# Two heads of a pair on row and column halves of the PE array, in place of a block-diagonal q and full-array numerators

## The chip, the cores and the metric

The kernel runs on one core of one Trainium2 chip. The metric is the time of one execution on the device in microseconds (us), lower is better. Engines are named as the profile names them: PE is TensorE (matmuls), PEld its weight loads, DVE is VectorE, ACT is ScalarE, POOL is GpSimd, SP is SyncE. All runs compared here are of the state that the measurement calls fast. Each kernel was run next to the kernel before on the same chip, and the comparison is by the ratio of the two.

## The reference, cut to what matters

Eight batches of eight heads, 576 tokens, head width 64. Attention is a band of 32 tokens to each side plus 8 global tokens; behind it comes an MLP with a snake activation.

```python
B, H, S, D = 8, 8, 576, 64                         # n_global = 8, window = 32
scores = q @ k^T / sqrt(D)                         # masked: |i-j| <= 32, or i or j global
attn   = softmax(scores)
x      = (attn @ v) as (B*S, 512)
h      = x @ w_in                                  # 512 -> 2048
g      = h + sin(alpha*h)**2 / alpha
out    = g @ w_out                                 # 2048 -> 512
```

## The kernel before

Work goes in chunks. For chunk `p` an *attention stretch* computes batch `p`, and carries the second-MLP matmuls (64 of 512 columns) of the chunk before as filling. Then a *first-MLP stretch* computes `w_in` and the activation for chunk `p`; it also holds the transposes of k and q for the first two head pairs of the next batch. An attention stretch has eight units: four head pairs `hp` times two halves `hf` of the sequence. A half has `NU` = 6 windows of `QC` = 56 query columns (48 own, 8 global) against 128 key rows.

Both heads of a pair (2 x 64 rows) share one matmul on the full 128 x 128 array. Scores need the heads apart, so q is stored block-diagonally (`qBD`: head 0 in rows 0 to 63, zeros below it, and so on), and ACT fills it with two 64-partition copies:

```python
for t in range(2):                                  # stage_T: q of one head pair
    pr = slice(64 * t, 64 * t + 64)
    nc.scalar.copy(out=qBD[hp][pr, :, t, 0:QB], in_=Qps[pr]...)

for u in range(NU):                                 # stage_Q: scores, 6 matmuls of 112 columns
    nc.tensor.matmul(out=Sp[:, u // HU, o : o + 2 * QC],
                     lhsT=kTw[hp][:, hf * NU + u, :], rhs=qBD[hp][:, hf * NU + u, :, :], ...)
E = exp(Sp) on ACT; E *= MASK on DVE

for t, on in enumerate((ones0, ones1)):             # stage_D: 2 accumulating matmuls of 336
    nc.tensor.matmul(out=den, lhsT=on[:], rhs=E[.., t, :], start=(t == 0), stop=(t == 1))
lnd = Ln(den); rec = Exp(-lnd) on ACT; gd = sum of den's global columns on DVE

num = psA.tile([P, 2, CH], F32, name="num")         # stage_V: two PSUM banks
for u in range(NU):                                 # 6 matmuls of 112 columns
    nc.tensor.matmul(out=num[:, u // HU, o : o + 2 * QC],
                     lhsT=W[:, .., hp * P : (hp + 1) * P], rhs=E[:, u // HU, o : o + 2 * QC], ...)
for t in range(2):                                  # the useful half of num, head by head
    nc.vector.tensor_tensor(out=xT[pr, hp, ...], in0=numv[pr, :, :, t, 0:QB], in1=rec[pr]..., op=mult)
nc.vector.tensor_reduce(out=gn, in_=numv[..., QB:QC], op=add)
```

The order of issue:

```python
# for each unit j: first(j) = scores(j+2), denominators(j+1); second(j) = numerators(j)
counts = [2, 0, 1, 0] + [1, 0] * NUN    # MLP slots (4 matmuls) behind each first/second
# next batch's transposes, as extras of the first-MLP slots 10 and 13:
i_ = (10, 13)
```

The matmuls write to eight banks of PSUM, the accumulator memory: two are held throughout (`Kps`, `ops`); the other six are shared in turn by the attention tiles and by the six `hb` tiles of the first MLP.

The softmax here doesn't subtract the row's maximum and nothing guards it: scores larger than these inputs give would overflow.

Of the kernel before, what the change touches and what calls it, by code (L numbers as in the profile page):

```python
# [12 lines left out]
ALU = mybir.AluOpType  # L13
# [5 lines left out]
def kernel(  # L19
# [11 lines left out]
    nc = tc.nc  # L31
    P = 128
    BF = DT.bfloat16
    F32 = DT.float32
# [32 lines left out]


    identb = const.tile([P, P], BF, name="identb")
    ones0 = const.tile([P, P], BF, name="ones0")  # L70
    ones1 = const.tile([P, P], BF, name="ones1")
    MASK = const.tile([P, NW, QC], BF, name="MASK")
    w_in = const.tile([P, CT, DFF], BF, name="w_in")
    w_out = const.tile([P, NT, DM], BF, name="w_out")
# [1 line left out]
    recipT = const.tile([P, NT], F32, name="recipT")  # L76
    xT = const.tile([P, CT, NTOK], BF, name="xT")
    kTw = [const.tile([P, NW, P], BF, name=f"kTw{i}") for i in range(NHP)]
    qBD = [const.tile([P, NW, 2, QC], BF, name=f"qBD{i}") for i in range(NHP)]
    VW = [const.tile([P, 2, NU, DM], BF, name=f"VW{i}") for i in range(2)]  # L80
    GT = const.tile([P, 2, NHP, B, NG], BF, name="GT")
    VgN = const.tile([NG * B, DM], BF, name="VgN")
# [63 lines left out]
    def zero(ap):  # L146
        nc.vector.memset(ap, 0.0)
# [52 lines left out]

    for hp in range(NHP):
        zero(kTw[hp][:, :, KB:P])
        zero(qBD[hp][:].rearrange("p i t c -> p (i t c)").bitcast(F32))
    zero_v(1)
    zero(ones0[:])
    zero(ones1[:])
    nc.vector.memset(ones0[:, 0:64], 1.0)
    nc.vector.memset(ones1[:, 64:128], 1.0)

    gN = [setup.tile([NG * B, DM], F32, name=f"gN{i}") for i in range(3)]  # L210
    halves = ((nc.sync, range(0, NG // 2)), (nc.scalar, range(NG // 2, NG)))
# [84 lines left out]
    def globals_in(b, hp, eng=nc.gpsimd):  # L296
        eng.tensor_copy(
            out=kTw[hp][:, :, KB : KB + NG],
            in_=GT[:, 0, hp, b, None, :].to_broadcast([P, NW, NG]),
        )  # L300
        for t in range(2):
            pr = slice(64 * t, 64 * t + 64)
            eng.tensor_copy(
                out=qBD[hp][pr, :, t, QB:QC],
                in_=GT[pr, 1, hp, b, None, :].to_broadcast([64, NW, NG]),
            )

    def stage_T(b, hp, qpool, qtag):
        QS, KS = qk[b]
        for jt in range(NTW):  # L310
            nc.tensor.transpose(
                out=Kps[:, WIN + jt * TW : WIN + (jt + 1) * TW],
                in_=KS[:, jt, 2 * hp : 2 * hp + 2, :],
                identity=identb[0:TW, 0:TW],
            )
        base = Kps[:, 0:1]
        nc.vector.tensor_copy(
            out=kTw[hp][:, :, 0:KB],
            in_=bass.AP(
                tensor=base.tensor, offset=base.offset,  # L320
                ap=[list(base.ap[0]), [QB, NW], [1, KB]],
            ),
        )
        Qps = qpool.tile([P, S], BF, name=qtag)
        for jt in range(NTW):
            nc.tensor.transpose(
                out=Qps[:, jt * TW : (jt + 1) * TW],
                in_=QS[:, jt, 2 * hp : 2 * hp + 2, :],
                identity=identb[0:TW, 0:TW],
            )  # L330
        for t in range(2):
            pr = slice(64 * t, 64 * t + 64)
            nc.scalar.copy(  # L333
                out=qBD[hp][pr, :, t, 0:QB],
                in_=Qps[pr].rearrange("p (i c) -> p i c", c=QB),
            )

    HU = NU // 2
    EW = HU * 2 * QC

    def stage_Q(psA, b, hp, hf):
        Sp = psA.tile([P, 2, CH], F32, name="Sp")
        for u in range(NU):
            o = (u % HU) * 2 * QC
            nc.tensor.matmul(  # L345
                out=Sp[:, u // HU, o : o + 2 * QC],
                lhsT=kTw[hp][:, hf * NU + u, :],
                rhs=qBD[hp][:, hf * NU + u, :, :],
                start=True, stop=True, skip_group_check=True,
            )  # L350
        E = epool.tile([P, 2, EW], BF, name="E")
        nc.scalar.activation(out=E[:], in_=Sp[:, :, 0:EW], func=AF.Exp, scale=scale)  # L352
        Ev = E[:].rearrange("p a (u t c) -> p (a u) t c", t=2, c=QC)
        nc.vector.tensor_tensor(  # L354
            out=Ev, in0=Ev,
            in1=MASK[:, hf * NU : (hf + 1) * NU, None, :].to_broadcast([P, NU, 2, QC]),
            op=ALU.mult,
        )
        return E

    def stage_D(psA, hp, hf, E, gd):
        den = psA.tile([P, NU, QC], F32, name="den")
        for t, on in enumerate((ones0, ones1)):
            nc.tensor.matmul(  # L364
                out=den[:].rearrange("p u c -> p (u c)"),
                lhsT=on[:],
                rhs=E[:].rearrange("p a (u t c) -> p (a u) t c", t=2, c=QC)[:, :, t, :],
                start=(t == 0), stop=(t == 1),
            )
        lnd = rpool.tile([P, NU, QB], F32, name="lnd", bufs=2)  # L370
        nc.scalar.activation(out=lnd[:], in_=den[:, :, 0:QB], func=AF.Ln)  # L371
# [8 lines left out]

    def stage_V(psA, b, hp, hf, E, rec, gn):
        W = VW[b % 2]
        num = psA.tile([P, 2, CH], F32, name="num")
        for u in range(NU):
            o = (u % HU) * 2 * QC
            i = hf * NU + u
            nc.tensor.matmul(  # L387
                out=num[:, u // HU, o : o + 2 * QC],
                lhsT=W[:, i % 2, i // 2, hp * P : (hp + 1) * P],
                rhs=E[:, u // HU, o : o + 2 * QC],  # L390
                start=True, stop=True, skip_group_check=True,
            )
        numv = num[:, :, 0:EW].rearrange("p a (u t c) -> p a u t c", t=2, c=QC)
        x0 = b * S + hf * NU * QB
        for t in range(2):
            pr = slice(64 * t, 64 * t + 64)
            nc.vector.tensor_tensor(  # L397
                out=xT[pr, hp, x0 : x0 + NU * QB].rearrange(
                    "p (a u c) -> p a u c", a=2, u=HU
                ),  # L400
                in0=numv[pr, :, :, t, 0:QB],
                in1=rec[pr].rearrange("p (a u) c -> p a u c", a=2),
                op=ALU.mult,
            )
        nc.vector.tensor_reduce(  # L405
            out=gn[:, hf, hp],
            in_=numv[:, :, :, :, QB:QC].rearrange("p a u t c -> p t c a u"),
            axis=mybir.AxisListType.XY, op=ALU.add,
        )

    def stage_Gd(gd, gr):
# [3 lines left out]
    def stage_G(b, gn, gr):  # L415
        gs = gpool.tile([P, NHP, NG], F32, name="gs")
        xg = gpool.tile([P, NHP, NG], BF, name="xg")
        for t in range(2):
            pr = slice(64 * t, 64 * t + 64)
            nc.vector.tensor_tensor(  # L420
                out=gs[pr], in0=gn[pr, 0, :, t], in1=gn[pr, 1, :, t], op=ALU.add
            )
        nc.vector.tensor_tensor(out=xg[:], in0=gs[:], in1=gr[:], op=ALU.mult)  # L423
        for j in range(NG):
            nc.gpsimd.tensor_copy(  # L425
                out=xT[:, :, b * S : (b + 1) * S][:, :, bass.ds(pregs[j], 1)],
                in_=xg[:, :, j : j + 1],
            )
# [4 lines left out]
    def attention(b, psA, t_at):  # L433

        Es, recs = {}, {}
        gn = gpool.tile([P, 2, NHP, 2, NG], F32, name="gn")
        gd = gpool.tile([P, 2, NHP, NG], F32, name="gd")
        gr = gpool.tile([P, NHP, NG], F32, name="gr")

# [231 lines left out]
```

## Time and profile before

| | before |
|---|---|
| median time | 419.77 us (419.44 to 419.98, 3 runs) |
| profiled span | 416.7 us |
| PE, DVE, ACT, POOL busy | 83%, 67%, 67%, 62% |
| first attention stretch, no filling | 33.1 us |
| a later round (attention + first MLP) | 41.6 us |

The page of the kernel before: first the busy time of each engine, then groups of instructions, with count, busy time and the mean of one.

```profile
PE 347.9 (83%) x2440; PEld 183.4 (44%) x2440; DVE 279.4 (67%) x636; ACT 277.1 (67%) x469; POOL 258.1 (62%) x418
...
L397 DVE TENSOR_TENSOR xT<-num,rec 64x288 bf16<-64x288 f32 x128 | 58.0, 453 | 8.7 <-PE num L387 6.8
...
L345 PE MATMUL Sp<-qBD,kTw 128*128 128x112 bf16 x384 | 31.1, 220 | 14.0 <-ACT E L352 11.1
L387 PE MATMUL num<-E,VW 128*128 128x112 bf16 x384 | 30.4, 217 | 11.0 <-DVE gn L405 8.1
L333 ACT COPY qBD<-qp 64x576 bf16<-64x576 bf16 x40 | 25.1, 627 | 18.6 <-DMA gN<-in_v_dram 13.7
```

The product into `xT` runs 128 times on 64 of 128 partitions, and PE waits 8.1 us in all for the `gn` sum that frees the numerator bank.

The timelines of one unit of a later attention stretch, PE first, then DVE. Columns: start, length, engine, line, what, count.

```profile
177.56 0.45 PE L364 MATMUL den<-E,ones 128*128 128x336 bf16 x2
177.84 1.02 PE L518 MATMUL ops<-w_out,H2b 128*128 128x512 bf16 x4
178.71 0.46 PE L387 MATMUL num<-E,VW 128*128 128x112 bf16 x6
179.00 0.46 PE L345 MATMUL Sp<-qBD,kTw 128*128 128x112 bf16 x6
179.34 0.45 PE L364 MATMUL den<-E,ones 128*128 128x336 bf16 x2
```

```profile
178.66 0.51 DVE L354 TENSOR_TENSOR E<-E,MASK 128x672 bf16<-128x672 bf16 x1
179.09 0.20 DVE L374 TENSOR_REDUCE gd<-den 128x8 f32<-128x48 f32 x1
179.20 0.92 DVE L397 TENSOR_TENSOR xT<-num,rec 64x288 bf16<-64x288 f32 x2
180.16 0.26 DVE L405 TENSOR_REDUCE gn<-num 128x16 f32<-128x96 f32 x1
180.45 0.61 DVE L354 TENSOR_TENSOR E<-E,MASK 128x672 bf16<-128x672 bf16 x1
```

Read starts, not lengths, on PE: matmuls overlap. From denominators to denominators it is 1.78 us, and from mask to mask on DVE it is 1.79 us with no idle time listed on DVE. PE and DVE are balanced here.

The handover from a first-MLP stretch to the next attention stretch, in PE's timeline:

```profile
202.61 1.89 PE L481 MATMUL hb<-xT,w_in 128*128 128x512 bf16 x8
204.33 0.46 PE L345 MATMUL Sp<-qBD,kTw 128*128 128x112 bf16 x6
204.63 1.89 PE L518 MATMUL ops<-w_out,H2b 128*128 128x512 bf16 x8
207.48 0.46 PE L345 MATMUL Sp<-qBD,kTw 128*128 128x112 bf16 x6 [0.96 <-ACT E L352]
208.37 0.45 PE L364 MATMUL den<-E,ones 128*128 128x336 bf16 x2 [0.43 <-DVE E L354]
```

Scores follow the first MLP at once; later PE waits 0.96 + 0.43 us for exp and mask. The mask itself follows four `H2b` products of DVE (the last step of the activation) without a gap.

### The profile page before, as it was taken

To read this page: it belongs to the slowest core of one execution; us is meant where nothing else is said; L and a number is where in the kernel's file an instruction comes from. 1 tells how busy PE (TensorE), PEld (TensorE's weight loads), DVE (VectorE), ACT (ScalarE), POOL (GpSimd) and SP (SyncE) were. 2 spreads that over 40 slices of the span, in tenths; PEclk is the share of its full clock that TensorE was granted. 3 is DMA by queue.
4 is the path that set the end of the run, shared out by engine and by line. 5 is a ranking of instruction groups with operands and counts; after the bars stand their busy time and mean duration, and the time that the engine had idled before them with its cause. 6 is when DMAs were issued, how large, how long until landed. Compare 5 with 4: busy or idle time off the path is not lost.

```text
span 416.7 us, 7242 instructions
## 1 busy us (share of the span) xinstructions
PE 347.9 (83%) x2440; PEld 183.4 (44%) x2440; DVE 279.4 (67%) x636; ACT 277.1 (67%) x469; POOL 258.1 (62%) x418
## 2 busy tenths in 40 slices
PE   1236399894978998899899989998999899989996
PEld 0124234552435544554455445544554454434442
DVE  7937649494687849784978497849784977484330
ACT  1156467893899578957894799479947994755421
POOL 8942097143988068956895689568956600685510
PEclk9999889998899999999999999999999999999999
DMA  6999899451999040993099309930994001000112
GB/s 54 142 160 200 137 83 156 70 55 30 155 127 135 33 115 4 136 114 101 3 139 114 99 3 141 114 96 3 143 111 97 2 25 52 25 2 26 53 51 76
DMA packets 133719, 35.22 MB, mean 85 GB/s; under 512 B 123314, under 2 KB 128178, under 8 KB 133682
## 3 DMA queue, kind: packets, MB, share of 16 engines
q0 software_dynamic: 122560, 19.02, 63.9%
q1 hardware_dynamic: 8034, 15.54, 12.9%
q10 hardware_dynamic: 3088, 0.21, 0.7%
q8 instruction: 19, 0.31, 0.3%
q14 instruction: 18, 0.15, 0.1%
HBM read 38.42 MB, written 9.44 MB: 115 GB/s over the span
## 4 chain that ended last, share of the span: by engine, by line
PE 42%; ACT 18%; DVE 17%; issue 11%; POOL 10%; POOLq 1%; ACTq 0%
PE hb L481 15%; PE ops L518 13%; ACT Sb L488 7%; DVE H2b L471 6%; PE den L518 5%; DVE xT L397 5%; ACT qBD L333 4%; DVE E L354 3%; POOL S L496 3%; PE num L387 2%; ACT S L494 2%; PE den L364 2%; DVE gn L405 2%; PE hb L518 2%; ACT E L352 2%
## 5 line engine op out<-in xcount | busy, mean ns | idle before, releaser
L481 PE MATMUL hb<-xT,w_in 128*128 128x512 bf16 x576 | 137.5, 387 | 11.0 <-POOL xT L425 8.3
L471 DVE SCALAR_TENSOR_TENSOR H2b<-S,recipT,hb 128x512 bf16<-128x512 bf16 x144 | 101.3, 742 | 48.5 <-POOL S L496 48.5
L488 ACT ACTIVATE Sb<-hb,alphaT 128x512 bf16<-128x512 f32 x144 | 94.1, 685 | 39.6 <-PE hb L481 36.1
L518 PE MATMUL ops<-w_out,H2b 128*128 128x512 bf16 x448 | 112.5, 379 | 7.0 <-ACT osb L525 6.5
L496 POOL TENSOR_TENSOR S<-Sb 128x512 bf16<-128x512 bf16 x91 | 94.4, 1064 | 38.4 <-ACT Sb L488 33.6
L481 PEld LDWEIGHTS <-w_in 128*128 128x128 bf16 x576 | 56.8, 99 | 83.0 <-issue 24.0
L518 PEld LDWEIGHTS <-H2b 128*128 128x128 bf16 x576 | 54.4, 97 | 63.6 <-issue 9.3
L397 DVE TENSOR_TENSOR xT<-num,rec 64x288 bf16<-64x288 f32 x128 | 58.0, 453 | 8.7 <-PE num L387 6.8
L352 ACT ACTIVATE E<-Sp 128x672 bf16<-128x672 f32 x64 | 46.8, 731 | 14.3 <-PE Sp L345 13.3
L425 POOL COPY xT<-xg 128x4 bf16 x64 | 13.0, 203 | 69.7 <-DVE xg L423 66.3
L354 DVE TENSOR_TENSOR E<-E,MASK 128x672 bf16<-128x672 bf16 x64 | 32.6, 511 | 24.4 <-ACT E L352 23.4
L108 POOL DMA_DIRECT2D VW<-in_v_dram x56 | 42.4, 766 | 0.7 <-PE num L387 0.3
L345 PE MATMUL Sp<-qBD,kTw 128*128 128x112 bf16 x384 | 31.1, 220 | 14.0 <-ACT E L352 11.1
L387 PE MATMUL num<-E,VW 128*128 128x112 bf16 x384 | 30.4, 217 | 11.0 <-DVE gn L405 8.1
L333 ACT COPY qBD<-qp 64x576 bf16<-64x576 bf16 x40 | 25.1, 627 | 18.6 <-DMA gN<-in_v_dram 13.7
L387 PEld LDWEIGHTS <-VW 128*128 128x128 bf16 x384 | 23.0, 100 | 31.9 <-DVE gn L405 21.9
L496 DVE TENSOR_TENSOR S<-Sb 128x512 bf16<-128x512 bf16 x37 | 17.6, 476 | 28.9 <-ACT Sb L488 28.2
L525 ACT COPY osb<-ops 128x512 f32<-128x512 f32 x28 | 16.3, 582 | 27.8 <-PE ops L518 27.2
L364 PE MATMUL den<-E,ones 128*128 128x336 bf16 x128 | 30.1, 318 | 5.5 <-DVE E L354 3.9
L345 PEld LDWEIGHTS <-kTw 128*128 128x128 bf16 x384 | 24.5, 102 | 20.9 <-issue 13.9
L371 ACT ACTIVATE lnd<-den 128x288 f32<-128x288 f32 x64 | 26.1, 408 | 6.9 <-PE den L364 6.4
L373 ACT ACTIVATE rec<-lnd 128x288 f32<-128x288 f32 x64 | 28.3, 443 | 2.0
(73 smaller groups left out, 344.4 us busy)
## 6 DMA issues: line engine op xcount, KB each, us to landing
out_dram<-osb SPq DMA_DIRECT2D x36, 256.0 KB
VW<-in_v_dram POOLq DMA_DIRECT2D x40, 112.0 KB, 4.8
VW<-VW SPq DMA_DIRECT2D x8, 384.0 KB
KS<-in_k_dram POOLq DMA_DIRECT2D x30, 96.0 KB, 4.0
QS<-in_q_dram POOLq DMA_DIRECT2D x30, 96.0 KB, 4.0
w_in<-in_moe_w_in_dram POOLq DMA_DIRECT2D x4, 512.0 KB, 8.5
w_out<-in_moe_w_out_dram POOLq DMA_DIRECT2D x4, 512.0 KB, 14.8
VW<-VW SPq DMA_DIRECT2D x8, 240.0 KB
```

What stands on the lines that cost most here:

```text
L108: nc.gpsimd.dma_start(out=W[p0 : p0 + n, par, u, :].rearrange("p (h d) -> p h d", d=D), in_=v[b, :, key0 : key0 + n, :].rearrange("h p d - ...
L333: nc.scalar.copy(out=qBD[hp][pr, :, t, 0:QB], in_=Qps[pr].rearrange("p (i c) -> p i c", c=QB),)
L345: nc.tensor.matmul(out=Sp[:, u // HU, o : o + 2 * QC], lhsT=kTw[hp][:, hf * NU + u, :], rhs=qBD[hp][:, hf * NU + u, :, :], start=True, sto ...
L352: nc.scalar.activation(out=E[:], in_=Sp[:, :, 0:EW], func=AF.Exp, scale=scale)
L354: nc.vector.tensor_tensor(out=Ev, in0=Ev, in1=MASK[:, hf * NU : (hf + 1) * NU, None, :].to_broadcast([P, NU, 2, QC]), op=ALU.mult,)
L387: nc.tensor.matmul(out=num[:, u // HU, o : o + 2 * QC], lhsT=W[:, i % 2, i // 2, hp * P : (hp + 1) * P], rhs=E[:, u // HU, o : o + 2 * QC] ...
L397: nc.vector.tensor_tensor(out=xT[pr, hp, x0 : x0 + NU * QB].rearrange("p (a u c) -> p a u c", a=2, u=HU), in0=numv[pr, :, :, t, 0:QB], in1 ...
L471: nc.vector.scalar_tensor_tensor(out=H2b[:, n_, :], in0=s_[:], scalar=recipT[:, n_ : n_ + 1], in1=h_, op0=ALU.mult, op1=ALU.add,)
L481: nc.tensor.matmul(out=h2[:], lhsT=w_in[:, ci, nt * P : (nt + 1) * P], rhs=xT[:, ci, c * CH : (c + 1) * CH], start=(ci == 0), stop=(ci == ...
L488: nc.scalar.activation(out=Sb[:], in_=h2[:], func=AF.Sin, scale=alphaT[:, nt : nt + 1])
L496: eng.tensor_tensor(out=S2[:], in0=Sb[:], in1=Sb[:], op=ALU.mult)
L518: nc.tensor.matmul(out=ops[:], lhsT=H2b[:, nt, ts * P : (ts + 1) * P], rhs=w_out[:, nt, :], start=(nt == 0), stop=(nt == NT - 1),)
```

## The change

The intent: each head works on its own half of the array. Scores contract over 64 rows, so the two heads run on two *row* halves and q needs no zeros and one copy. Denominators and numerators of a head are 64 columns wide, so the two heads run on two *column* halves; the numerators of both then lie in the same columns of one PSUM bank, and one 128-partition product fills `xT`.

```diff
-    ones0, ones1 = const.tile([P, P]) twice, half zeros, half ones
-    qBD = [const.tile([P, NW, 2, QC], BF, ...)]
+    ones = const.tile([P, 64], BF, name="ones")
+    qT = [const.tile([P, NW, QC], BF, ...)]
 ... stage_T
-        for t in range(2):
-            nc.scalar.copy(out=qBD[hp][pr, :, t, 0:QB], in_=Qps[pr]...)
+        nc.scalar.copy(out=qT[hp][:, :, 0:QB], in_=Qps[:]...)
 ... stage_Q
-            nc.tensor.matmul(out=Sp[:, u // HU, o : o + 2 * QC],
-                lhsT=kTw[hp][:, hf * NU + u, :], rhs=qBD[hp][:, hf * NU + u, :, :], ...)
+            for t, pr in heads:                       # pr: partitions 64t to 64t+63
+                nc.tensor.matmul(out=Sp[:, t, u * QC : (u + 1) * QC],
+                    lhsT=kTw[hp][pr, i, :], rhs=qT[hp][pr, i, :], ...)
 ... stage_D
-        for t, on in enumerate((ones0, ones1)):
-            nc.tensor.matmul(out=den, lhsT=on[:], rhs=E[.., t, :], start=(t == 0), stop=(t == 1))
+        for t, pr in heads:
+            nc.tensor.matmul(out=den[pr], lhsT=ones[:], rhs=E[:, t, :], start=True, stop=True, ...)
 ... stage_V
-        num = psA.tile([P, 2, CH], F32, name="num")
+        num = psA.tile([P, NU, QC], F32, name="num")
-            nc.tensor.matmul(out=num[:, u // HU, o : o + 2 * QC],
-                lhsT=W[:, .., hp * P : (hp + 1) * P], rhs=E[:, u // HU, o : o + 2 * QC], ...)
+            for t, pr in heads:
+                nc.tensor.matmul(out=num[pr, u, :],
+                    lhsT=W[:, .., c0 : c0 + 64], rhs=E[:, t, u * QC : (u + 1) * QC], ...)
-        for t in range(2):
-            nc.vector.tensor_tensor(out=xT[pr, hp, ...], in0=numv[pr, :, :, t, 0:QB], ...)
+        nc.vector.tensor_tensor(out=xT[:, hp, ...], in0=num[:, :, 0:QB], in1=rec[:], op=ALU.mult)
 ... (the sums of the global columns shrink alike; schedule and buffer counts are unchanged)
```

More of the change, by code (lines that the diff above doesn't have):

```diff
@@ L69 @@
     identb = const.tile([P, P], BF, name="identb")
-    ones0 = const.tile([P, P], BF, name="ones0")
-    ones1 = const.tile([P, P], BF, name="ones1")
+    ones = const.tile([P, 64], BF, name="ones")
     MASK = const.tile([P, NW, QC], BF, name="MASK")
@@ L78 @@
     kTw = [const.tile([P, NW, P], BF, name=f"kTw{i}") for i in range(NHP)]
-    qBD = [const.tile([P, NW, 2, QC], BF, name=f"qBD{i}") for i in range(NHP)]
+    qT = [const.tile([P, NW, QC], BF, name=f"qT{i}") for i in range(NHP)]
     VW = [const.tile([P, 2, NU, DM], BF, name=f"VW{i}") for i in range(2)]
@@ L202 @@
         zero(kTw[hp][:, :, KB:P])
-        zero(qBD[hp][:].rearrange("p i t c -> p (i t c)").bitcast(F32))
     zero_v(1)
-    zero(ones0[:])
-    zero(ones1[:])
-    nc.vector.memset(ones0[:, 0:64], 1.0)
-    nc.vector.memset(ones1[:, 64:128], 1.0)
+    nc.vector.memset(ones[:], 1.0)
     gN = [setup.tile([NG * B, DM], F32, name=f"gN{i}") for i in range(3)]
@@ L300, in globals_in @@
         )
-        for t in range(2):
-            pr = slice(64 * t, 64 * t + 64)
-            eng.tensor_copy(
-                out=qBD[hp][pr, :, t, QB:QC],
-                in_=GT[pr, 1, hp, b, None, :].to_broadcast([64, NW, NG]),
-            )
+        eng.tensor_copy(
+            out=qT[hp][:, :, QB:QC],
+            in_=GT[:, 1, hp, b, None, :].to_broadcast([P, NW, NG]),
+        )
     def stage_T(b, hp, qpool, qtag):
@@ L330, in stage_T @@
             )
-        for t in range(2):
-            pr = slice(64 * t, 64 * t + 64)
-            nc.scalar.copy(
-                out=qBD[hp][pr, :, t, 0:QB],
-                in_=Qps[pr].rearrange("p (i c) -> p i c", c=QB),
-            )
-    HU = NU // 2
-    EW = HU * 2 * QC
+        nc.scalar.copy(
+            out=qT[hp][:, :, 0:QB], in_=Qps[:].rearrange("p (i c) -> p i c", c=QB)
+        )
+    EW = NU * QC
+    heads = [(t, slice(64 * t, 64 * t + 64)) for t in range(2)]
     def stage_Q(psA, b, hp, hf):
@@ L343, in stage_Q @@
         for u in range(NU):
-            o = (u % HU) * 2 * QC
-            nc.tensor.matmul(
-                out=Sp[:, u // HU, o : o + 2 * QC],
-                lhsT=kTw[hp][:, hf * NU + u, :],
-                rhs=qBD[hp][:, hf * NU + u, :, :],
-                start=True, stop=True, skip_group_check=True,
-            )
+            i = hf * NU + u
+            for t, pr in heads:
+                nc.tensor.matmul(
+                    out=Sp[:, t, u * QC : (u + 1) * QC],
+                    lhsT=kTw[hp][pr, i, :], rhs=qT[hp][pr, i, :],
+                    start=True, stop=True, skip_group_check=True,
+                )
         E = epool.tile([P, 2, EW], BF, name="E")
         nc.scalar.activation(out=E[:], in_=Sp[:, :, 0:EW], func=AF.Exp, scale=scale)
-        Ev = E[:].rearrange("p a (u t c) -> p (a u) t c", t=2, c=QC)
+        mk = MASK[:, hf * NU : (hf + 1) * NU, :].rearrange("p u c -> p (u c)")
         nc.vector.tensor_tensor(
-            out=Ev, in0=Ev,
-            in1=MASK[:, hf * NU : (hf + 1) * NU, None, :].to_broadcast([P, NU, 2, QC]),
-            op=ALU.mult,
+            out=E[:], in0=E[:], in1=mk[:, None, :].to_broadcast([P, 2, EW]), op=ALU.mult
         )
@@ L362, in stage_D @@
         den = psA.tile([P, NU, QC], F32, name="den")
-        for t, on in enumerate((ones0, ones1)):
+        for t, pr in heads:
             nc.tensor.matmul(
-                out=den[:].rearrange("p u c -> p (u c)"),
-                lhsT=on[:],
-                rhs=E[:].rearrange("p a (u t c) -> p (a u) t c", t=2, c=QC)[:, :, t, :],
-                start=(t == 0), stop=(t == 1),
+                out=den[pr].rearrange("p u c -> p (u c)"),
+                lhsT=ones[:], rhs=E[:, t, :],
+                start=True, stop=True, skip_group_check=True,
             )
@@ L382, in stage_V @@
         W = VW[b % 2]
-        num = psA.tile([P, 2, CH], F32, name="num")
+        num = psA.tile([P, NU, QC], F32, name="num")
         for u in range(NU):
-            o = (u % HU) * 2 * QC
             i = hf * NU + u
-            nc.tensor.matmul(
-                out=num[:, u // HU, o : o + 2 * QC],
-                lhsT=W[:, i % 2, i // 2, hp * P : (hp + 1) * P],
-                rhs=E[:, u // HU, o : o + 2 * QC],
-                start=True, stop=True, skip_group_check=True,
-            )
-        numv = num[:, :, 0:EW].rearrange("p a (u t c) -> p a u t c", t=2, c=QC)
-        x0 = b * S + hf * NU * QB
-        for t in range(2):
-            pr = slice(64 * t, 64 * t + 64)
-            nc.vector.tensor_tensor(
-                out=xT[pr, hp, x0 : x0 + NU * QB].rearrange(
-                    "p (a u c) -> p a u c", a=2, u=HU
-                ),
-                in0=numv[pr, :, :, t, 0:QB],
-                in1=rec[pr].rearrange("p (a u) c -> p a u c", a=2),
-                op=ALU.mult,
-            )
+            for t, pr in heads:
+                c0 = hp * P + 64 * t
+                nc.tensor.matmul(
+                    out=num[pr, u, :],
+                    lhsT=W[:, i % 2, i // 2, c0 : c0 + 64],
+                    rhs=E[:, t, u * QC : (u + 1) * QC],
+                    start=True, stop=True, skip_group_check=True,
+                )
+        x0 = b * S + hf * NU * QB
+        nc.vector.tensor_tensor(
+            out=xT[:, hp, x0 : x0 + NU * QB].rearrange("p (u c) -> p u c", u=NU),
+            in0=num[:, :, 0:QB], in1=rec[:], op=ALU.mult,
+        )
         nc.vector.tensor_reduce(
-            out=gn[:, hf, hp],
-            in_=numv[:, :, :, :, QB:QC].rearrange("p a u t c -> p t c a u"),
-            axis=mybir.AxisListType.XY, op=ALU.add,
+            out=gn[:, hf, hp, :],
+            in_=num[:, :, QB:QC].rearrange("p u c -> p c u"),
+            axis=mybir.AxisListType.X, op=ALU.add,
         )
@@ L417, in stage_G @@
         xg = gpool.tile([P, NHP, NG], BF, name="xg")
-        for t in range(2):
-            pr = slice(64 * t, 64 * t + 64)
-            nc.vector.tensor_tensor(
-                out=gs[pr], in0=gn[pr, 0, :, t], in1=gn[pr, 1, :, t], op=ALU.add
-            )
+        nc.vector.tensor_tensor(out=gs[:], in0=gn[:, 0], in1=gn[:, 1], op=ALU.add)
         nc.vector.tensor_tensor(out=xg[:], in0=gs[:], in1=gr[:], op=ALU.mult)
@@ L435, in attention @@
         Es, recs = {}, {}
-        gn = gpool.tile([P, 2, NHP, 2, NG], F32, name="gn")
+        gn = gpool.tile([P, 2, NHP, NG], F32, name="gn")
         gd = gpool.tile([P, 2, NHP, NG], F32, name="gd")
```

## The prediction

> **What bounds the kernel now.** From batch 2 on, the trace repeats every 41.6 us: an attention stretch of 22.6 us that also carries the 64 second-MLP matmuls of the chunk before, then a first-MLP stretch of 19.0 us. The table of stretches for 166.3 to 188.9 us gives PE 20.6 us busy, DVE 16.7, ACT 15.1: this stretch is bound by PE, with some 2 us of gaps. In the timeline one attention unit (half a head pair) costs PE 0.30 us for six score matmuls (49 ns apart), 0.29 us for two denominators, 0.30 us for six numerators, and 0.86 us for four MLP matmuls: 1.75 us. The DVE chain per unit is as long: mask 0.51, denominator sums 0.20, two xT products 0.92, numerator sums 0.26, with handovers 1.78 us (three units in a row in the chain of waits). So PE and DVE are balanced, and relieving DVE alone cannot gain more than PE's gaps.
>
> **What the change removes.** DVE: one 64-partition xT product of 453 ns in each of 64 units, and half of the numerator sum (258 to about 200 ns): 0.51 us a unit, 33 us in all. ACT: one of two q copies of 627 ns, 32 times, 20 us. Setup: four memsets of 618 ns.
>
> **What it does on PE.** The denominators become two column halves; if they run at once, 0.29 becomes about 0.15 us. Scores and numerators become twelve matmuls of 56 columns, each with its own weight load, in place of six of 112: at best half the time, but I estimate 25 to 45 ns each (transposes of 96 columns are 43 ns apart, the closest pace in the trace), so 0.3 to 0.5 us, no gain. The Trainium skill, "TensorE: Matmul & The Clock Gate", Part 3, says that matmuls on different row or column groups run concurrently; no trace here shows it yet. "TensorEngine Tiling (Array Packing)", Key Properties, says that changing the tiling mode drains TensorE. A unit would change mode four times (scores, denominators, MLP, numerators), 32 times a stretch. The trace has one hint of the price: after the 64-row transposes of the globals the next matmul starts 0.27 us later, against 0.05 us between equals, at a cold clock and perhaps for other reasons. I estimate 0.03 to 0.2 us a switch, most likely near 0.08: +2.6 us a stretch.
>
> **On the critical path.** In the seven attention stretches with MLP work: PE's gaps (2 us) mostly go, denominators give back about 1 us, switches and more instructions take 2 to 4 us: about zero, from -3 to +4 us each. In the first-MLP stretches the chain of waits shows two q copies (0.52 + 0.22 us) near the end; one goes, about 0.6 us in six stretches, -4 us. The first attention stretch, without MLP work, follows the DVE and ACT chain: -2 to -4 us; setup up to -2 us.
>
> **Prediction:** 413 us, 8 in 10 between 394 and 440. Faster by over 2%: 0.43; within 2%: 0.29; slower by over 2%: 0.28.
>
> **What would show it.** xT products 64, near 455 ns, on 128 partitions; q copies 32, near 630 ns; DVE about 12.5 us in an attention stretch. On PE: pairs with nearly equal starts if halves are concurrent; a gap at each change of mode; more "issue" and PE in the chain of waits, DVE's xT nearly gone from it.
>
> **What would make it wrong.** Switches near 0.2 us or 64-column weight loads slower than the 56-column matmuls: 440 us or more. Free switches with real concurrency: below 398 us.

## The result, and the profile after

The kernel after takes 403.76 us (402.37 to 404.39, 4 runs) against 419.72 us for the kernel before: ratio 0.9615, 95% interval 0.9587 to 0.9644. A ratio in this document is the mean time of one kernel's fast runs over that of the other's fast runs of the same rounds, so it is not quite the ratio of the quoted medians. The gain is 16 us, 3.85%: inside the stated range, but over twice the 1.6% forecast.

Groups of the kernel after, from its page:

```profile
PE 341.6 (85%) x3157; PEld 169.6 (42%) x3208; DVE 236.1 (59%) x549; ACT 256.4 (64%) x437; POOL 250.9 (63%) x394
...
L336 PE MATMUL Sp<-qT,kTw 64*128 64x56 bf16 x768 | 22.2, 191 | 16.7 <-DVE H2b L448 11.5
L382 DVE TENSOR_TENSOR xT<-num,rec 128x288 bf16<-128x288 f32 x64 | 29.1, 455 | 11.1 <-PE num L375 7.5
...
L375 PE MATMUL num<-E,VW 128*64 128x56 bf16 x768 | 25.3, 201 | 2.5 <-DVE gn L386 1.4
```

The `xT` products are 64 at 455 ns, as forecast: a product on 128 partitions costs what one on 64 cost. DVE's busy time falls by 43 us and ACT's by 21 us. The wait of the numerators for `gn` is nearly gone. But the scores have a new wait, 11.5 us, for `H2b`.

The timelines of a unit, PE, then DVE:

```profile
203.65 0.33 PE L336 MATMUL Sp<-qT,kTw 64*128 64x56 bf16 x12
203.91 0.33 PE L352 MATMUL den<-E,ones 128*64 128x336 bf16 x2
204.17 1.04 PE L495 MATMUL ops<-w_out,H2b 128*128 128x512 bf16 x4
205.14 0.38 PE L375 MATMUL num<-E,VW 128*64 128x56 bf16 x12
205.45 0.33 PE L336 MATMUL Sp<-qT,kTw 64*128 64x56 bf16 x12
```

```profile
204.78 0.51 DVE L344 TENSOR_TENSOR E<-E,MASK 128x672 bf16<-128x672 bf16 x1 [0.44 <-ACT E L342]
205.21 0.20 DVE L361 TENSOR_REDUCE gd<-den 128x8 f32<-128x48 f32 x1
205.56 0.46 DVE L382 TENSOR_TENSOR xT<-num,rec 128x288 bf16<-128x288 f32 x1
205.93 0.20 DVE L386 TENSOR_REDUCE gn<-num 128x8 f32<-128x48 f32 x1
206.58 0.51 DVE L344 TENSOR_TENSOR E<-E,MASK 128x672 bf16<-128x672 bf16 x1 [0.45 <-ACT E L342]
```

A unit still takes 1.80 us, though PE's score, denominator and numerator streams were halved on paper. DVE now sits idle 0.44 us before each mask: PE alone sets the pace.

Where PE's halved work went shows in the starts of single matmuls. These are the usual values in both traces where nothing else was waited for (medians; for denominators to MLP after, the lower quartile, as many of those MLP matmuls also waited). "A to b" is from the last start of group a to the first start of group b:

| step of a unit, ns | before | after |
|---|---|---|
| scores, first to last start | 246 (6) | 146 (12) |
| scores to denominators | 49 | 113 |
| denominators, first to last start | 141 | 3 |
| denominators to MLP | 142 | 262 |
| numerators, first to last start | 246 (6) | 183 (12) |
| numerators to scores | 49 | 125 |
| last MLP matmul to numerators | 216 | 309 |
| sum | 1089 | 1141 |

The halves do run at once: the two heads' matmuls start 3 ns apart, and from the start of one pair to the start of the next it is mostly 25 to 26 ns for scores and 31 to 32 ns for numerators. The two denominators start 3 ns apart. So the packing works better than I had estimated. But the changes of array mode, four in a unit, add some 0.1 us each where the stream before them is the same: last MLP matmul to numerators is 309 against 216 ns (+93), with the same stream before it; denominators to MLP is 262 against 142 (+120). In sum the steps of a unit cost PE 52 ns more than before. For the change as a whole the gain is not in PE's own work.

The handover of a later round, PE's timeline of the kernel after:

```profile
189.81 1.89 PE L458 MATMUL hb<-xT,w_in 128*128 128x512 bf16 x7
193.54 0.33 PE L336 MATMUL Sp<-qT,kTw 64*128 64x56 bf16 x12 [1.85 <-DVE H2b L448]
193.81 1.90 PE L495 MATMUL ops<-w_out,H2b 128*128 128x512 bf16 x8
195.64 0.33 PE L336 MATMUL Sp<-qT,kTw 64*128 64x56 bf16 x12
```

PE stands idle for 1.85 us for the DVE line that frees an `hb` bank. In the kernel before there was no such wait; there PE went on with the eight MLP matmuls. The placement of tiles in banks, which I read from the built programs, tells why (the traces show the wait, not the bank): the score tile has banks 2 and 3 in both. Before, bank 3 was last used by the second q transposes, which ACT's copies free early. After, the fourteenth `hb` tile and those transposes have changed places (banks 3 and 6), and that `hb` tile is freed only by its `H2b` product. No line of the diff mentions it.

Stage by stage, from the first matmuls of each stretch (a round is from one first-MLP start to the next):

| part | before | after | difference |
|---|---|---|---|
| start to first scores | 19.8 | 20.0 | +0.2 |
| first attention stretch (no filling) | 33.1 | 26.6 | -6.5 |
| round 1 | 48.9 | 45.6 | -3.3 |
| round 2 | 45.8 | 43.2 | -2.6 |
| rounds 3 to 7 together | 207.5 | 203.5 | -4.0 |
| last first-MLP start to the end | 61.6 | 61.6 | 0 |

The sum is 16.2 us. Over a third comes from the first stretch. Nearly all that the seven rounds gain lies in their attention stretches: from the first denominators to the next first-MLP start they are 1.0 to 2.6 us shorter each, 11.4 us together. From the first-MLP start to the first denominators rounds 1 and 2 gain 0.7 and 0.9 us, but rounds 3 to 5 and 7 lose 0.3 to 0.5 us each (round 6, with a slower clock that is explained under e9, 1.7 us).

### The profile page after: what moved, and what is told of

It reads as the page before. It is cut to its first block, busy times and chain, and to the rows that moved or that the text cites. A ratio compares the mean times of both kernels' runs of the same rounds, so it can differ in the third digit from the quotient of the medians.

```text
span 400.5 us, 8548 instructions
## 1 busy us (share of the span) xinstructions
PE 341.6 (85%) x3157; PEld 169.6 (42%) x3208; DVE 236.1 (59%) x549; ACT 256.4 (64%) x437; POOL 250.9 (63%) x394
## 4 chain that ended last, share of the span: by engine, by line
PE 50%; POOL 14%; ACT 12%; issue 11%; DVE 11%; POOLq 1%; ACTq 0%
PE ops L495 23%; PE hb L458 8%; ACT Sb L465 7%; DVE H2b L448 7%; POOL S L473 7%; PE den L495 5%; PE num L375 4%; PE Sp L336 3%; PE den L352 3%; DVE kTw L310 2%; ACT S L471 2%; PE hb L495 2%; POOL KS L95 2%; POOL QS L95 1%; POOL VW L107 1%
## 5 line engine op out<-in xcount | busy, mean ns | idle before, releaser
L458 PE MATMUL hb<-xT,w_in 128*128 128x512 bf16 x559 | 134.9, 387 | 10.1 <-POOL xT L402 6.6
L495 PE MATMUL ops<-w_out,H2b 128*128 128x512 bf16 x414 | 109.3, 383 | 4.1 <-issue 1.3
L495 PEld LDWEIGHTS <-H2b 128*128 128x128 bf16 x576 | 51.4, 98 | 60.3 <-issue 8.9
L342 ACT ACTIVATE E<-Sp 128x672 bf16<-128x672 f32 x64 | 46.8, 732 | 19.9 <-PE Sp L336 19.2
L336 PE MATMUL Sp<-qT,kTw 64*128 64x56 bf16 x768 | 22.2, 191 | 16.7 <-DVE H2b L448 11.5
L382 DVE TENSOR_TENSOR xT<-num,rec 128x288 bf16<-128x288 f32 x64 | 29.1, 455 | 11.1 <-PE num L375 7.5
L375 PEld LDWEIGHTS <-VW 128*64 128x64 bf16 x768 | 18.5, 116 | 27.9 <-issue 14.7
L310 DVE COPY kTw<-Kps 128x1344 bf16<-128x1344 bf16 x32 | 27.2, 850 | 3.0 <-PE Kps L304 3.0
L375 PE MATMUL num<-E,VW 128*64 128x56 bf16 x768 | 25.3, 201 | 2.5 <-DVE gn L386 1.4
L336 PEld LDWEIGHTS <-kTw 64*128 64x128 bf16 x768 | 15.8, 96 | 27.4 <-issue 23.7
L352 PE MATMUL den<-E,ones 128*64 128x336 bf16 x128 | 22.7, 347 | 5.1 <-DVE E L344 3.3
```

Source lines behind the costliest of these rows:

```text
L310: nc.vector.tensor_copy(out=kTw[hp][:, :, 0:KB], in_=bass.AP(tensor=base.tensor, offset=base.offset, ap=[list(base.ap[0]), [QB, NW], [1, KB]],
L336: nc.tensor.matmul(out=Sp[:, t, u * QC : (u + 1) * QC], lhsT=kTw[hp][pr, i, :], rhs=qT[hp][pr, i, :], start=True, stop=True, skip_group_ch ...
L342: nc.scalar.activation(out=E[:], in_=Sp[:, :, 0:EW], func=AF.Exp, scale=scale)
L352: nc.tensor.matmul(out=den[pr].rearrange("p u c -> p (u c)"), lhsT=ones[:], rhs=E[:, t, :], start=True, stop=True, skip_group_check=True,)
L375: nc.tensor.matmul(out=num[pr, u, :], lhsT=W[:, i % 2, i // 2, c0 : c0 + 64], rhs=E[:, t, u * QC : (u + 1) * QC], start=True, stop=True, s ...
L458: nc.tensor.matmul(out=h2[:], lhsT=w_in[:, ci, nt * P : (nt + 1) * P], rhs=xT[:, ci, c * CH : (c + 1) * CH], start=(ci == 0), stop=(ci == ...
```

## The experiments

The theory: on PE the packing and its changes of mode cancel; the gain is DVE's and ACT's shorter work; and part of it is lost again to the new bank wait. The main rivals: the gain is packed matmuls; the bank wait is harmless because ACT's chain ends last there. The kernel after has ratio 0.9615 to before; each run below has its ratio to before too, from runs on the same chip.

| run | median us | ratio to before, 95% interval |
|---|---|---|
| after | 403.76 | 0.9615 (0.9587 to 0.9644) |
| e7 after, two xT products | 410.42 | 0.9793 (0.9761 to 0.9825) |
| e6 after, denominators on the full array | 404.72 | 0.9634 (0.9594 to 0.9674) |
| e4 after, one more change of mode a unit | 410.34 | 0.9799 (0.9777 to 0.9821) |
| e11 row halves only | 413.97 | 0.9866 (0.9831 to 0.9901) |
| e12 column halves only | 412.40 | 0.9842 (0.9813 to 0.9872) |
| e1 after, two q copies in first MLP | 400.03 | 0.9544 (0.9527 to 0.9561) |
| e2 after, first transposes a slot later | 399.16 | 0.9531 (0.9514 to 0.9548) |
| e3 after, MLP matmuls before scores | 398.00 | 0.9505 (0.9485 to 0.9526) |
| e13 before, same order as e3 | 419.59 | 0.9999 (0.9981 to 1.0016) |
| e5 after, MLP behind numerators | 404.25 | 0.9649 (0.9629 to 0.9669) |
| e8 e3 and e5 together | 401.05 | 0.9572 (0.9550 to 0.9593) |
| e9 e5, numerators in two banks | 403.10 | 0.9619 (0.9591 to 0.9646) |
| e10 e9 and e3 together | 393.29 | 0.9386 (0.9356 to 0.9415) |
| e14 e10 with e2 and a split filling | 396.10 | 0.9445 (0.9429 to 0.9461) |

All fourteen gave correct results.

### e7: give DVE its second product back

```diff
-        nc.vector.tensor_tensor(out=xT[:, hp, ...], in0=num[:, :, 0:QB], in1=rec[:], op=ALU.mult)
+        for t, pr in heads:
+            nc.vector.tensor_tensor(out=xT[pr, hp, ...], in0=num[pr, :, 0:QB], in1=rec[pr], op=ALU.mult)
```

> The kernel after, but the product into xT is again two VectorE instructions of 64 partitions, 0.455 us each; PE's work is as in after. Theory (the gain of the change comes from VectorE's shorter chain, PE's sum being even): VectorE per unit 0.51 + 0.20 + 0.92 + 0.20 us is again as long as PE's 1.80; 0.5 to 1.5 us more in each stretch and 2 to 3 us in the first one, 408 to 416 us. Rival (the gain comes from packing on PE, VectorE has slack): below 406 us.

Ratio 0.9793: about 7.5 us (0.0178 of 419) of the 16 are gone with this one line. DVE's timeline in that kernel has no idle time before the mask:

```profile
212.46 0.51 DVE L344 TENSOR_TENSOR E<-E,MASK 128x672 bf16<-128x672 bf16 x1
...
213.01 0.91 DVE L383 TENSOR_TENSOR xT<-num,rec 64x288 bf16<-64x288 f32 x2
213.95 0.21 DVE L387 TENSOR_REDUCE gn<-num 128x8 f32<-128x48 f32 x1
214.19 0.51 DVE L344 TENSOR_TENSOR E<-E,MASK 128x672 bf16<-128x672 bf16 x1
```

The first attention stretch, up to the first-MLP start, is 3.8 us longer than in after (50.38 against 46.60 us from the start). Rounds 1 and 2 together are 2.8 us longer, a spell of slow clock (see e9) included. DVE's relief is shown as a cause worth 7.5 us, about half of it in the first stretch. It is not shown to be the largest: e12 below, which leaves out the row half, loses 9.5 us against after.

### e6: denominators on the full array again

```diff
-        for t, pr in heads:
-            nc.tensor.matmul(out=den[pr], lhsT=ones[:], rhs=E[:, t, :], start=True, stop=True, ...)
+        for t in range(2):
+            nc.tensor.matmul(out=den, lhsT=onesh[t][:], rhs=E[:, t, :], start=(t == 0), stop=(t == 1))
```

> The kernel after, but the denominators are again two accumulating full-array matmuls with half-filled ones. From the trace of after, last score matmul to first MLP matmul takes 113 + 3 + 262 = 378 ns; undone it should be about 115 + 141 + 142 = 398 ns. Theory (packing saves as much PE time as its change of mode costs): within 2 us of after, 402 to 406 us. Rival (packing the denominators is a gain of 0.14 us a unit, 9 us): 411 to 413 us.

Ratio 0.9634, not to be told from after. In the trace the second denominator matmul starts 154 ns (median) after the first in place of 3, and denominators to MLP takes 142 in place of 262 (one change of mode less). Halving these matmuls bought nothing that the times show.

### e4: one more change of mode

```diff
-    G4 = 4 ; counts = [2, 0, 1, 0] + [1, 0] * (NUN)
+    G4 = 2 ; counts = [4, 0, 2, 0] + [1, 1] * (NUN)      # two MLP matmuls behind each half of a unit
```

> The kernel after, but the second-MLP matmuls of an attention unit come as two groups of two (one behind the denominators, one behind the numerators) and not as one group of four: five changes of array mode in a unit in place of four, the same matmuls. Theory (a change of mode costs PE about 0.1 us, measured in after from start to start as 92 to 121 ns over the stream, and the stretch is bound by PE): 56 units with one change more, +5 to +6 us, 408 to 411 us. Rival (the gap at a change is hidden, or is only the wait for another engine): within 1.5 us of after.

Ratio 0.9799, 7.7 us over after. Of that, 2.1 us are behind the last first-MLP start (63.69 against 61.60 us), where the smaller groups also changed the order, and do not count. A later round at full clock takes 41.21 us against 40.3 to 40.4: 0.8 to 0.9 us for eight changes more, 0.1 us each. The price of a change of mode is shown twice, from starts and by adding one. Removing one is not worth as much, as e5 to e10 show.

### e11 and e12: each half of the change alone

e11 takes the row half into the kernel before (scores, one q copy), e12 the column half (denominators, numerators, one `xT` product):

```diff
# e11, against before              # e12, against before
+ qT, scores on row halves         + den[pr], num[pr] on column halves, one bank
+ one q copy of 128 partitions     + one xT product, gn with 8 columns
  den, num as before               qBD, scores, two q copies as before
```

> The kernel before with only the row half of the change: scores from two row halves, one q copy, no block-diagonal q; denominators and numerators on the full array, two xT products. Its second q transposes and fourteenth hidden tile have the banks of after. Theory (gain from VectorE's relief; PE even): scores save 0.12 us a unit and two changes of mode cost 0.19, VectorE as before, the new wait for H2b appears; little gain, from the first stretch and ScalarE, 414 to 421 us. Rival (gain from ScalarE's q copy and from the packed scores): 409 to 412 us.

> The kernel before with only the column half of the change: denominators and numerators in column halves, one-bank numerators, one xT product, scores from the block-diagonal q on the full array, two q copies. Banks as in before, so no new wait for H2b. A unit changes mode three times (full to column, column to full, twice: four). Theory (gain from VectorE's relief): most of the gain of the change, 404 to 410 us, with PE's unit some 0.03 us dearer or cheaper than in before. Rival (the gain needs the packed scores and ScalarE): 413 us or more.

The rows alone gain 1.3%, the columns alone 1.6%; together they gain 3.85%. e12 missed its expectation; e11, at 413.97 us, came out at the lower edge of its own. Two things hold e12 back. The first is PE itself: it changes mode four times a unit, as after does, but without the short scores. Its steps, summed as in the table above, are 1270 ns (before 1089, after 1141, e11 1164), and a unit where PE waits for nothing takes 1.94 us (after 1.80). So once the columns are split, splitting the rows takes 0.13 us off PE's unit: the two halves share the price of the changes. The second is ACT, with its two q copies ahead of each `osb` copy (the results of the second MLP). PE's waits for `osb`, in before, e12 and e11 (waited in all, times, longest):

```profile
PE ops L518 <- ACT osb L525: 5.6, 7, 0.8
PE ops L504 <- ACT osb L511: 4.1, 7, 0.7
PE ops L511 <- ACT osb L518: 0.2, 1, 0.2
```

With one q copy this wait is gone, in after too: the unit that held it took 2.73 us in the later rounds of before and 1.84 in after, the largest single saving of such a round. No run puts back the q copies of the attention stretches or the wide scores alone, so their shares of e12's 9.5 us are not separated. In e11 PE still waits 3.4 us for `gn` and 1.9 us for `gd`, so DVE stays a brake. Relief of one engine leaves the other in the way, and this with the shared changes of mode is why the halves do not add up. e11 has the new 11.5 us wait for `H2b`, e12 has not, as the expectations said of their banks.

### e1, e2, e3: three ways around the bank wait

```diff
# e1: in the first-MLP stretches two q copies again; this alone restores the old bank placement
-        nc.scalar.copy(out=qT[hp][:, :, 0:QB], in_=Qps[:]...)
+        for t, pr in (heads if qtag == "hb" else [(0, slice(0, P))]):
+            nc.scalar.copy(out=qT[hp][pr, :, 0:QB], in_=Qps[pr]...)
# e2
-                i_ = (10, 13)
+                i_ = (11, 13)
# e3, before the parts of a stretch run
+                if p > 1:
+                    chain(*fill[:2])                     # eight second-MLP matmuls
+                    fill, counts = fill[2:], [0] + counts[1:]
```

> The kernel after, but in the first-MLP stretches the q copy is again two 64-partition copies on ScalarE; all else as in after. With it the built program gives the second q transposes bank 3 and the fourteenth hidden tile bank 6, as in the kernel before. Theory (new bank wait): the score matmuls' wait for the DVE line that writes H2b, 11.5 us over six stretches in after, vanishes, and although ScalarE works 7.5 us more the kernel gets faster, 398 to 401 us (the before's start of the second score group, 18.7 us after the first-MLP start against 19.6 in after). Rival (the wait is harmless because ScalarE's table load and exp end last there): 404 us or slower, up to 409.

> The kernel after, but the first head pair's transposes are issued one slot later in the first-MLP stretch (slot 11 in place of 10). With it the score tile's two banks are last used by slot 11 and by the second transposes, not by slot 13. Theory (new bank wait): the 11.5 us of waits of the score matmuls for H2b shrink below 2 us, and 6 to 11 us come off: 393 to 398 us. Rival (harmless wait): 403 to 405 us.

> The kernel after, but from batch 2 on the first eight second-MLP matmuls of an attention stretch stand before the first score group instead of behind it, so that PE has work while the score bank is not free. Theory (the bank wait leaves PE idle in a stretch that PE bounds): PE's wait for H2b falls from 1.9 to near 0.2 us a stretch; the second score group then waits about 0.8 us for the first exp; net 0.8 to 1.7 us for each of six stretches, 394 to 399 us. Rival (harmless): 403 to 405 us.

All three are faster than after. In e1 an undone saving (ACT works more) makes the kernel faster, because it moves a tile to another bank. What PE waits for from 69 to 345 us, first in after, then in e1, then in e3 (waited in all, times, longest):

```profile
PE Sp L336 <- DVE H2b L448: 11.5, 6, 2.3
```

```profile
PE Sp L337 <- ACT E L343: 7.6, 7, 1.8
PE den L353 <- DVE E L345: 3.5, 7, 0.6
```

```profile
PE Sp L336 <- ACT E L342: 5.6, 7, 0.8
...
PE den L352 <- DVE E L344: 1.7, 7, 0.3
```

The wait for `H2b` goes, but waits for exp and mask take most of its place (11.1 us in e1, 7.8 in e2, 7.3 in e3). So the bank wait's net cost in e1 and e2 is some 0.3 to 0.4 us a round (40.3 to 40.4 down to 40.0 and 40.1), not the 1 to 2 us that I expected: e2's 393 to 398 us was a miss at 399.16. e3 has rounds of 39.7 us.

### e13: the same order in the kernel before

The edit is that of e3.

> The kernel before with the first reordering (eight second-MLP matmuls ahead of the first score group from batch 2 on). Theory (the reordering pays in after because PE idles there for a bank that the change took away): the kernel before had no such wait, only 1.4 us of waits for exp and mask behind the MLP matmuls, and these grow when the MLP matmuls stand in front; no gain, 418 to 424 us. Rival (the reordering is good for any kernel): 412 to 415 us.

Ratio 0.9999. The kernel before cannot gain from this order, so e3's gain mends what the change brought about.

### e5, e9, e8, e10: fewer changes of mode

```diff
# e5: denominators and numerators (both column halves) follow each other
-                    counts = [2, 0, 1, 0] + [1, 0] * (NUN)
+                    counts = [2, 0, 1, 0] + [0, 1] * (NUN)
# e9: e5, and the bank that the change freed
-        num = psA.tile([P, NU, QC], F32, name="num")
+        num = psA.tile([P, NU, QC], F32, name="num", bufs=2)
# e8 = e5 + e3 ; e10 = e9 + e3
```

> The kernel after, but the four second-MLP matmuls of an attention unit come behind the numerators and not before them, so that denominators and numerators, both in column halves, follow each other: three changes of array mode in a unit in place of four. Theory (a change costs PE 0.09 to 0.12 us and PE bounds these stretches): 0.7 to 0.9 us off each of seven stretches, 5 to 7 us, 396 to 399 us. Rival (the numerators now come too early and wait for the numerator bank or for the reciprocals, or the gap is hidden): 402 to 406 us.

> The kernel of the run with the MLP matmuls behind the numerators, which did not get faster, with the numerator tile in two banks in turn (the change freed one). In that run the numerators started 0.34 to 0.38 us after the denominators in place of some 0.15, when VectorE had just read the numerators before. Theory (three changes of mode save PE time, but the single numerator bank took it back): that gap falls to about 0.16 us and 5 to 7 us come off, to 395 to 399 us. Rival (the gap at the change of mode is not what costs): 402 us or more.

> Both reorderings: the first eight second-MLP matmuls before the first score group, and the MLP matmuls of a unit behind its numerators. Theory: the two gains are of different places (idle PE at the start of a stretch; three changes of mode a unit) and add up: 5 to 7 us below the kernel with the first reordering alone, 390 to 394 us. Rival: they share the same slack and the sum is no more than 2 us better than the better one.

> All three: first eight MLP matmuls before the first score group, MLP matmuls behind the numerators, numerator tile in two banks in turn. Theory: both gains add, 389 to 393 us, the fastest of all. Rival: 395 us or more, no better than the first reordering alone.

e5 gained nothing. In its trace the numerators start 337 to 475 ns (the middle half of the cases) after the denominators, although no change of mode lies between: with the MLP matmuls gone from there, they come before DVE has read the numerators of the unit before. e8, with the same single bank, has the same late numerators (352 to 475 ns) and is slower than e3 alone; it missed the 390 to 394 us of its theory. In e9, with two banks, that gap is 163 ns, yet e9 gained nothing either: a miss with another cause. The granted clock shows it. These are stretches of e9 (busy times of PE, PEld, DVE, ACT, POOL, then PEclk): the end of a first MLP with the idle wait, and the start of the attention stretch (the last two columns are DMA).

```profile
187.00:191.90 4.90, 3.06 (x23) 1.53 (x22) 4.90 (x9) 4.17 (x6) 3.88 (x4) 1.00 0.00 0
191.90:196.00 4.10, 4.09 (x35) 1.66 (x35) 1.69 (x3) 1.53 (x3) 4.10 (x7) 0.63 0.99 65
```

After the 1.84 us that PE idles for the bank, its clock is halved for 3.41 us, and the eight MLP matmuls take 2.84 us in place of 1.90. This happened in four of e9's seven filled stretches; among rounds 3 to 7 the ones with it take 41.6 to 41.7 us, the others 39.9 and 40.2. The profile of after has one such spell past 100 us (round 6, 41.85 us in place of 40.3), e6 has three, e11 two, e4 and e7 one, e5 none. The profiles of e1, e2, e3, e8, e10, e13 and e14, which do not idle that long there, have none past 110 us; e12 has one at 121.6 us, without the bank wait. That is one profiled execution of each kernel, but the traces of all sixteen say when it happens. In each of them all these spells begin on one grid of 3.41 us. I cut the time from 60 to 360 us into the windows of that grid and left out those already at half clock. With 2.07 us or more of PE idle (by the profile's modelled ends) in a window the next one was at half clock in 20 cases of 20, with 1.81 to 1.85 us in 9 of 16, with 1.70 us or less in none of 1315. A bank wait of 1.84 us that falls into one window lies at that edge, so it costs clock in some rounds and not in others; cut by the border of two windows, as all six of e5 are, it costs none. The mean clocks agree for e9 and e10: 0.979 in all four runs of e9, 0.996 in all four of e10, where the wait is filled and 9.8 us came off (403.10 to 393.29). e3's profile, with a clock of 0.994, is of its fastest run (395.60 us); its other three have 0.985 to 0.986 and 397.5 to 398.7 us, so more half-clock time occurs there too, and no trace shows where.

e10's handover and unit, PE's timeline: filling first, and no MLP matmul between denominators and numerators.

```profile
187.22 1.89 PE L495 MATMUL ops<-w_out,H2b 128*128 128x512 bf16 x8
189.23 0.33 PE L336 MATMUL Sp<-qT,kTw 64*128 64x56 bf16 x12
190.38 0.33 PE L336 MATMUL Sp<-qT,kTw 64*128 64x56 bf16 x12 [0.82 <-ACT E L342]
...
200.74 0.33 PE L352 MATMUL den<-E,ones 128*64 128x336 bf16 x2
200.90 0.35 PE L375 MATMUL num<-E,VW 128*64 128x56 bf16 x12
201.19 1.04 PE L495 MATMUL ops<-w_out,H2b 128*128 128x512 bf16 x4
...
202.42 0.33 PE L352 MATMUL den<-E,ones 128*64 128x336 bf16 x2
```

Denominators to denominators is now 1.68 us, against 1.80 in after. e10 is the fastest kernel, 6.1% below before and inside the interval of neither single reordering; 393.29 us is just above the 389 to 393 of its theory. The removed changes of mode pay only in part: against e3, with eight changes fewer in a stretch and a second bank, a later round is 39.43 in place of 39.7 us, a third of what eight times 0.1 us would be. Part of the 4.7 us between e3 and e10 is clock, as above.

### e14: fill the last gap too

```diff
# e10, and:
-                    chain(*fill[:2]) ; fill, counts = fill[2:], [0] + counts[1:]
+                    chain(fill[0])   ; fill, counts = fill[1:], [1] + counts[1:]
-                i_ = (10, 13)
+                i_ = (11, 13)
```

> The fastest kernel so far, but the first transposes one slot later (no wait for the bank) and only four MLP matmuls ahead of the first score group, the other four between the first and the second, where PE waited 0.8 us for the exp. Theory: 0.5 to 1 us less of PE idle in each of six stretches, 387 to 391 us. Rival (exp and ScalarE's chain bound this place, not PE): 392 to 395 us.

It is slower than e10 (0.9445 against 0.9386), and 396.10 us missed both ranges. The scores wait for no bank and start 17.0 us after the first-MLP start (17.6 in e10). But with the first transposes a slot later PE waits 0.40 us for DVE's `kTw` copy before the second transposes, and the last first-MLP matmul starts 0.5 us later. PE then waits for exp 0.79 us even behind the four MLP matmuls; the second scores come at 19.1 us against 18.7 in e10, the first denominators at 19.7 against 19.3. The rival is right that PE does not bound this place, but ACT is only half of it: in both kernels DVE's first mask, which the denominators wait for, follows DVE's four last `H2b` products without a gap. e14 changed two things at once; only the later transposes are seen to cost.

## Why the prediction was right or wrong

- **Bound (right).** PE and DVE were balanced at 1.78 us a unit, and the removed DVE and ACT work has the size named: 64 products at 455 ns, 32 q copies at about 628 ns.
- **Concurrency and changes of mode (right in kind).** The Trainium skill, "TensorE: Matmul & The Clock Gate", Part 3, gives about 4 ns between the starts of concurrent tiles; this trace has 3 ns. "TensorEngine Tiling (Array Packing)", Key Properties, says that a change of mode drains TensorE; measured at 93 to 120 ns, inside the estimated 0.03 to 0.2 us.
- **"About zero" for the seven attention stretches with MLP work, from "0.3 to 0.5 us, no gain" for scores and numerators (failed step).** The kind was right and this size was wrong. First to last start is 146 ns for twelve scores and 183 for twelve numerators, 13 and 17 ns from one start to the next on average, where I took 25 to 45 ns for each matmul. This saves 0.10 and 0.06 us a unit, which with 0.14 us on the denominators pays for most of the four changes: +0.05 us a unit, some 0.4 us a stretch, where "switches and more instructions take 2 to 4 us" less about 1 us had been put in. So the gaps of PE that "mostly go" (5.6 us of waits for `osb` among them) count nearly in full: 1.0 to 2.6 us a stretch, 11.4 us in seven, where about zero was forecast.
- **The first stretch, "-2 to -4 us" (mis-sized).** It was -6.5 us, of which e7 alone gives 3.8 us back: without filling nothing covers DVE and ACT. (Profiles of kernels with the same code up to there differ by about 1 us in it: 33.1 us in before, 34.3 in e13.)
- **"About 0.6 us in six" first-MLP stretches from ACT (failed too, in the other direction).** The saved copy moved a tile to another bank, and the next scores waited 1.84 to 2.28 us for `H2b`. The first denominators of a later round come 19.9 us after the first-MLP start in place of 19.6. Nothing in the prediction asked what a changed order of released buffers would do; e1, e2 and e3 show the loss. Even with the wait filled (e3, e10) they come at 19.3, where e13, before in the same order, has 19.6: half of the 0.6 us. In e10's trace DVE's `H2b` products and the mask behind them then end last.
- **Setup, "up to -2 us" (wrong).** The first scores start no earlier: at 20.0 us against 19.8, and 19.7 to 20.8 us in the other profiles of kernels with the new setup. The removed memsets were not seen to be on the way.
- **The total.** 413 us against 403.76. The mechanism was right in kind; the gains of the attention stretches were put too low, and the loss at the bank, 3.0 us by e1, was not foreseen. The two errors had opposite signs, so by luck the number is nearer than its terms.

## What to carry to other kernels

On halves of the PE array two 56-column matmuls followed each other every 26 to 32 ns, where one of 112 columns took 49, but each change of mode cost about 0.1 us. So group the work of one mode, give the tiles between them enough banks, and measure: eight changes fewer in a stretch saved 0.3 us a round (e10 against e3), not 0.8. A packed layout can pay elsewhere: here VectorE and ScalarE worked on 128 partitions in the time of 64 (455 against 453 ns, 626 to 630 against 627). After any change of instruction counts look at what the first instruction of each stage waits for: a pool may have placed tiles in other banks, and 1.8 us of PE idle within one window of 3.41 us can cost its clock as well.

## What the Trainium skill lacked or had wrong

- "TensorEngine Tiling (Array Packing)", Key Properties, says that a change of tiling mode drains TensorE but gives no price: here 93 to 120 ns from start to start over the same stream, and 0.1 us by adding one (e4).
- "TensorE: Matmul & The Clock Gate", Part 1, says that the distance between starts "never drops below ≈25 ns however small N is". The sentence makes no exception for tiles that run at once, which Part 3 of the same page has at about 4 ns. Here it was 3 ns within a pair and 25 to 26 ns from pair to pair, 13 ns a matmul on average, for twelve row-half matmuls of 56 columns with a weight load each.
- "TensorEngine Tiling (Array Packing)", Restrictions, says that column tiling switches off Fast Weight Load, without its cost. No run here shows which kind of load was used; a 64-column load into a column half took 116 ns in the after profile's groups against 96 ns for a 128-column load into a row half, and pairs of numerators followed each other every 31 to 32 ns, pairs of scores every 25 to 26.
- "TensorE: Matmul & The Clock Gate", Why this matters for your kernels, advises no PE-idle gaps over about 3 us. Here waits of 1.84 us and more were followed by 3.41 us at half clock in four of six stretches (e9). The length of the spells and their grid agree with the page's window of 3413 ns, but a gap was not safe up to 3 us: over all traces half clock followed windows with 1.81 to 1.85 us of PE idle in 9 cases of 16 and with 2.07 us or more in 20 of 20.
- No page tells that a saved instruction on ScalarE can change a pool's order of banks and so add a wait (1.84 to 2.28 us in each of six stretches here).
